# A new order for the first 12 blocks of an attention kernel: K is turned ahead of x, and q products stand between scores

## The chip, the cores and the metric

The kernel runs on one core of one Trainium2 chip. The metric is the device time of one execution in microseconds. "PE" is TensorE, "PEld" its weight loads, "DVE" VectorE, "ACT" ScalarE, "POOL" GpSimd, and "SP" SyncE, which here only issues DMAs.

## The reference

Everything is bf16 at the border, with 2048 tokens of width 640 and 32 heads of size 192. Only the last 512 keys and values of each head are used.

```python
xn = _layernorm(x)                                    # (1, 2048, 640)
q = (xn @ wq).reshape(1, 2048, 32, 192).transpose(0, 2, 1, 3)
k, v = k_cache[:, :, -512:, :], v_cache[:, :, -512:, :]
p = softmax(einsum("bhqd,bhkd->bhqk", q, k) * 192 ** -0.5)
o = einsum("bhqk,bhkd->bhqd", p, v)
s = o.transpose(0, 2, 1, 3).reshape(1, 2048, 6144) @ wo
g = silu(B(xn, w_r, w_gate, w_up, w_down))            # adds a gated FFN to the 2 tokens with the largest xn @ w_r
return x + s * g
```

## The kernel before

The 32 heads are processed in 8 groups of 4 (`GROUP`), and a group in two pairs of heads. The tokens come in four quads of 512, which are four tiles of 128 tokens each. A step is (group, quad, pair), and a step has two blocks of 256 tokens, so there are 128 blocks. One block needs:

- **q** (`q_whole`, line 302, or `q_phase`, line 323): the q of a step, transposed, in three parts (c = 0, 1, 2) of five products each, since 640 = 5 x 128. An eviction to `qT` on DVE (line 313) or ACT (lines 315, 350, 352) scales each part. `q_whole` uses all 128 rows of PE at once. `q_phase` and all the products below use 64-row halves, two at a time.
- **Scores** (`scores`, line 358): six products for one 128-token tile (a = 0 or 1) and both heads, `S` for short. The tile takes one of two PSUM buffers (`ps_s`).
- **Row maxima** (`row_max`, line 370, DVE) and **exponentials** (`exps`, line 375, ACT, one per head), `M` and `E`. A DMA on SP then transposes the exponentials into `pT`. A block whose number is in `SPLIT` (line 290) transposes each half by itself (line 381), another one both halves together after the second (line 383).
- **V products** (`o_item`, line 425): 32 products with `pT`, two evictions that divide by the row sums (lines 413 to 420, on the engines named, "v" for DVE and "a" for ACT), and a DMA transpose into `oT` (line 423). `P` for short.
- **Output products** (`w_item`, line 455): 24 products with `wo`, accumulated in `s_acc` (in the first group a copy, line 466 on ACT or 468 on DVE). `W` for short.

Before all of this, x is normalised. The first quad has tiles 0 to 3: statistics per half tile (`first_bn`, line 252), a square root on ACT (`first_dev`, 259), a reciprocal and the application on DVE (`first_apply`, 262). The later quads have `ln_parts` (line 486): statistics on DVE (`st`, line 496) or sums on ACT (`sa`, lines 507 and 511), then an inverse square root in steps (`nw`, lines 225 to 248: a logarithm and an exponential on ACT, one addition on POOL, three small steps on DVE, and the negated mean, line 197), and the application on ACT, DVE or POOL (`ap`, lines 189 to 194). Each tile is then turned by five PE products against an identity and evicted into `xnT` (`turn_tile`, line 279). The K of the first pair is turned on PE, too, in two parts of six products (`k_turn`, line 267). Later pairs have K reordered by a copy on POOL (`k_order`, line 118) and turned by a DMA (`k_transpose`, line 123). `wo` is loaded into one half of the partitions and doubled by a copy on POOL (`wo_double`, `wd`, line 148).

The order of all this is written out by hand: under `manual_schedule` (line 47) each engine executes its instructions in the order in which the program names them, and each DMA queue its DMAs. The kernel has 13 warming products on zeros (line 163). The first 12 blocks (`HEAD`, line 289) then follow the list of tokens `FIRST` (line 602), which `first` (line 528) carries out: `S.3.1` are the scores of block 3, tile 1, `q.2.1.a` is part 1 of step 2's q evicted on ACT, `P.1.va` the V products of block 1 with evictions on DVE and ACT, and so on. Blocks 12 and later follow one fixed pattern (`BLOCK`, line 946). The list ends with lines 999 to 1002.

The first loads stand ahead of the list: the first x tile and both heads' K on SP (lines 99 and 111), then x tiles 2 and 3 (line 157), and on ACT's queue x tile 1 and the first wq (lines 100 and 133).

## Time and profile before

| | us |
|---|---|
| median of 3 runs (lowest, highest) | 792.52 (791.92, 792.92) |
| the profiled execution | 793.03 |
| its span, first to last instruction | 791.3 |
| PE busy | 777.6 |
| DVE busy | 579.0 |
| ACT busy | 527.9 |
| POOL busy | 338.8 |

The profiled execution is one single execution, so its times belong together; it is 1.73 us longer than its span. Times in views of the trace count from the start of the span. In a timeline row the columns are start, duration, engine, line, operation, output<-inputs, number of instructions, and in brackets how long the engine was idle before it and what ended that. SPq and ACTq are issues of DMAs. A row of DMA issues has the queue, the number, the size of each, and the median time from issue to landing. A row of windows has the stretch and its length, the busy time of PE, PEld, DVE, ACT and POOL with the number of instructions, the granted clock of PE, the busy share of the DMA engines and GB/s.

### The profile page before, as it was taken

How to read it: one execution, taken by the hardware profiler on the slowest of the kernel's cores; microseconds unless marked ns; L12 is line 12 of the kernel's file. 1: busy time of each engine (PE TensorE's matmuls, PEld its weight loads, DVE VectorE, ACT ScalarE, POOL GpSimd, SP SyncE). 2: the span in 40 equal slices, each digit the busy share in tenths (PEclk: the TensorE clock that was granted, in tenths of full speed). 3: DMA queues.
4: the chain of work that ended last, by engine and by line, in shares of the span. 5: the costliest groups of instructions: out<-in, count | busy, mean ns of one | idle time of the engine just before them, and what ended most of it. 6: DMA issues, size and time to landing. Idle time of an engine off the chain costs nothing.

```text
span 791.3 us, 26980 instructions
## 1 busy us (share of the span) xinstructions
PE 777.6 (98%) x11356; PEld 571.5 (72%) x11356; DVE 579.0 (73%) x1069; ACT 527.9 (67%) x954; POOL 338.8 (43%) x280
## 2 busy tenths in 40 slices
PE   8899999999999999999999999999999999999997
PEld 4457677777777777777777777777777777777775
DVE  7898788877777776767776766766766766776775
ACT  5676666667666677767666666766666666666662
POOL 1334110023110226626120101569977795256895
PEclk9999999999999999999999999999999999999999
DMA  9989999899999999999999999999999999999992
GB/s 231 199 175 170 175 190 167 141 189 164 174 193 186 179 200 199 184 174 195 179 195 198 190 206 191 159 190 188 159 171 185 148 180 183 185 171 167 187 186 84
DMA packets 447130, 142.18 MB, mean 180 GB/s; under 512 B 414180, under 2 KB 446438, under 8 KB 447008
## 3 DMA queue, kind: packets, MB, share of 16 engines
q1 hardware_dynamic: 437312, 130.88, 99.7%
q10 hardware_dynamic: 8672, 6.72, 3.3%
q0 software_dynamic: 1024, 2.85, 1.3%
q8 instruction: 89, 1.46, 0.8%
q14 instruction: 33, 0.27, 0.1%
HBM read 40.31 MB, written 2.63 MB: 54 GB/s over the span
## 4 chain that ended last, share of the span: by engine, by line
PE 89%; DMA 4%; DVE 3%; ACT 2%; issue 1%; SPq 0%; DVEq 0%; ACTq 0%
PE w L447 24%; PE q_ps L340 23%; PE o_ps L406 20%; PE s L367 19%; DMA oT<-o_sb 2%; DVE nm L372 2%; ACT pexp L377 1%; PE q_ps L309 1%; DMA x_in<-in_A_x_dram 1%; DMA pT<-pexp 1%; DMA v_sb<-in_A_v_cache_dram 1%; DMA xsT<-xsel 0%; DVE fin_o L475 0%; PE tp L282 0%; PE gu_ps L787 0%
## 5 line engine op out<-in xcount | busy, mean ns | idle before, releaser
L372 DVE TENSOR_REDUCE nm<-s 128x2 f32<-128x1024 f32 x256 | 312.9, 1223 | 137.8 <-PE s L367 136.1
L377 ACT ACTIVATE pexp<-s,nm 128x512 bf16<-128x512 f32 x512 | 324.1, 688 | 95.3 <-DVE nm L372 91.0
L340 PE MATMUL q_ps<-xnT,wq_g 64*128 64x512 bf16 (+1 forms) x2340 | 232.4, 323 | 0.0
L447 PE MATMUL w<-wo_g,oT 64*128 64x320 bf16 x3072 | 231.5, 296 | 0.2
L367 PE MATMUL s<-kT,qT 64*128 64x512 bf16 x1536 | 211.4, 376 | 2.5 <-ACT pexp L377 1.7
L447 PEld LDWEIGHTS <-oT 64*128 64x128 bf16 x3072 | 169.1, 94 | 59.7 <-DMA oT<-o_sb 1.4
L406 PEld LDWEIGHTS <-pT 64*128 64x128 bf16 x4096 | 177.3, 94 | 31.4 <-issue 2.8
L406 PE MATMUL o_ps<-v_sb,pT 64*128 64x193 bf16 x4096 | 195.3, 243 | 2.9 <-DMA pT<-pexp 1.8
L420 ACT ACTIVATE o_sb<-o_ps,rl 128x192 bf16<-128x192 f32 x250 | 91.6, 418 | 133.6 <-DVE rl L413 128.3
L340 PEld LDWEIGHTS <-wq_g 64*128 64x128 bf16 x2340 | 125.5, 99 | 46.1 <-DVE qT L313 0.5
L151 POOL COPY wo_g<-wo_g 64x1920 bf16<-64x1920 bf16 x32 | 57.4, 1797 | 189.4 <-DMA wo_g<-in_A_wo_dram 188.5
L367 PEld LDWEIGHTS <-qT 64*128 64x128 bf16 x1536 | 84.5, 94 | 57.6 <-DVE qT L313 3.0
L470 DVE TENSOR_TENSOR s_acc<-s_acc,w 128x320 f32<-128x320 f32 x192 | 84.9, 484 | 31.8 <-PE w L447 31.7
L352 ACT ACTIVATE qT<-q_ps 128x1024 bf16<-128x1024 f32 x114 | 92.4, 811 | 7.4 <-PE q_ps L340 1.4
L417 DVE TENSOR_TENSOR o_sb<-o_ps,rl 128x384 bf16<-128x384 f32 x131 | 73.0, 557 | 4.5
L121 POOL COPY k_perm<-k_raw 128x768 bf16<-128x768 bf16 x30 | 24.2, 827 | 95.4 <-DMA k_raw<-in_A_k_cache_dram 68.7
L877 POOL TENSOR_SCALAR yh<-y_bc,oh 128x640 f32<-128x640 f32 x32 | 60.3, 1886 | 5.4 <-DMA y_bc<-y_d 2.6
L878 POOL TENSOR_TENSOR xn<-xn,yh 128x640 bf16<-128x640 bf16 x32 | 45.0, 1406 | 2.7
L864 POOL TENSOR_TENSOR tz<-tz,xn 128x640 f32<-128x640 f32 x16 | 22.4, 1400 | 54.2 <-ACT tz L863 54.2
L413 DVE RECIPROCAL rl<-o_ps 128x2 f32<-128x2 f32 x256 | 30.5, 160 | 12.2 <-PE o_ps L406 7.6
L937 POOL TENSOR_TENSOR s_acc<-s_acc,x_fin 128x640 f32<-128x640 f32 x16 | 22.4, 1400 | 11.0 <-DMA x_fin<-in_A_x_dram 10.1
L865 POOL TENSOR_TENSOR xn<-tz,xn 128x640 bf16<-128x640 f32 x16 | 22.4, 1398 | 1.3
(138 smaller groups left out, 275.9 us busy)
## 6 DMA issues: line engine op xcount, KB each, us to landing
wo_g<-in_A_wo_dram SPq DMA_DIRECT2D x32, 240.0 KB, 4.2
k_raw<-in_A_k_cache_dram SPq DMA_DIRECT2D x32, 192.0 KB, 3.3
v_sb<-in_A_v_cache_dram SPq DMA_DIRECT2D x32, 192.0 KB, 4.1
wq_g<-in_A_wq_dram SPq DMA_DIRECT2D x14, 288.0 KB, 3.7
pT<-pexp SPq DMA_TRANSPOSE x246, 4.2
wq_g<-in_A_wq_dram SPq DMA_DIRECT2D x14, 192.0 KB, 3.1
x_fin<-in_A_x_dram SPq DMA_DIRECT2D x16, 160.0 KB, 3.8
oT<-o_sb SPq DMA_TRANSPOSE x126, 3.6
```

What stands on the lines that cost most here:

```text
L151: nc.gpsimd.tensor_copy(out=grp[g][("wo", pr)][half(1), cs, :], in_=grp[g][("wo", pr)][half(0), cs, :])
L340: mm = nc.tensor.matmul(q_ps[k][:, 0:n] if type(q_ps) is list else q_ps[:, k, 0:n], lhsT=wq[half(r), dc, c:2 * Dh:3], rhs=xnT[half(r), tok ...
L352: nc.scalar.activation(out=out, in_=q_ps[:, :, 0:n], func=ACT.Copy, scale=scale)
L367: nc.tensor.matmul(s_of[b, a][:, r, :], lhsT=qT_of[i][half(r), c, u * P:(u + 1) * P], rhs=grp[g][("kT", pr)][half(r), :, c, :], start=(c = ...
L372: rm = nc.vector.tensor_reduce(out=nm_of[b, a], in_=s_of[b, a], axis=AX.X, op=ALU.max, negate=True)
L377: nc.scalar.activation(out=p_ring[:, b % 2, a, :, hh, :].rearrange("p (x j) e -> p x j e", x=2), in_=s_of[b, a][:, hh, :].rearrange("p (j ...
L406: nc.tensor.matmul(o_of[b][r][:, a, 0:Dh + 1], lhsT=pT_ring[half(r), b % RP, a, k, :], rhs=v_ring[half(r), (g * PAIRS + pr) % RV, k, 0:Dh ...
L417: nc.vector.tensor_tensor(out=o_sb, in0=src, in1=rl[:, r].unsqueeze(2).unsqueeze(3).to_broadcast([P, 2, 3, HK]), op=ALU.mult)
L420: nc.scalar.activation(out=o_sb[:, a], in_=src[:, a], func=ACT.Copy, scale=rl[:, r, a:a + 1])
L447: nc.tensor.matmul(w_ps[r][:, 0:HD], lhsT=oT_ring[half(r), bs[pr] % RT, c, :], rhs=grp[g][("wo", pr)][half(r), c, cs], start=(pr == 0 and ...
L470: nc.vector.tensor_tensor(out=acc, in0=acc, in1=src, op=ALU.add)
L877: nc.gpsimd.tensor_scalar(out=yh, in0=M["y_bc"][:, j, :], scalar1=M["oh"][:, n, j:j + 1], scalar2=None, op0=ALU.mult)
```

## The change

Only the first 12 blocks are touched. The first loads become tokens of the list (`lx`, `lk`, `lq`): SP issues x tiles 0, 2, 3 and wq, and ACT's queue x tile 1 and the two halves of K. In the list, K's turns (`kturn`) come ahead of the first two x tiles' turns. The statistics of tiles 2 and 3 come earlier. Many q products of steps 0 to 3, in parts of five, stand between two scores, where they stood in runs of 10 or 15 products. Evictions change engines: 4 of q, 2 of turned x tiles, 6 of the output products and one of two of a V product go from DVE to ACT; one application of the normalisation leaves ACT and one leaves DVE, and POOL takes both. Loads, copies and statistics stand at other places in the list, `wd.0` (the first doubling of `wo`) ahead of the last steps of the second quad's inverse square root among them. Whether a block's transposes are split is said by its token (`E.4.0.s`) and remembered in `split_of`: blocks 0 to 4 and 8 among the first 12, where it was 0 to 3; blocks 12 to 126 stay split. The number of products on each shape is the same.

```diff
@@ -96,8 +96,6 @@
         nc.sync.dma_start(out=x_in[t5][:, ts, :], in_=x_v[:, t5 * 4 + ts.start:t5 * 4 + ts.stop, :])
 
     x_in[0] = xin_pool.tile([P, 4, D], BF16, name="x_in")
-    nc.sync.dma_start(out=x_in[0][:, 0, :], in_=x_v[:, 0, :])
-    nc.scalar.dma_start(out=x_in[0][:, 1, :], in_=x_v[:, 1, :])
 
     grp = defaultdict(dict)
 
@@ -149,12 +147,6 @@
         pr, part = divmod(c, 2)
         cs = slice(part * 3, part * 3 + 3)
         nc.gpsimd.tensor_copy(out=grp[g][("wo", pr)][half(1), cs, :], in_=grp[g][("wo", pr)][half(0), cs, :])
-
-    for hh in range(2):
-        k_piece(0, 0, hh, nc.sync)
-    wq_piece(0, 0, 0, nc.scalar)
-    for n in (2, 3):
-        nc.sync.dma_start(out=x_in[0][:, n, :], in_=x_v[:, n, :])
 
     idle = late.enter_context(tc.tile_pool(name="idle", bufs=1)).tile([P, W], BF16, name="idle")
     nc.vector.memset(idle, 0.0)
@@ -287,7 +279,6 @@
     NS = len(steps)
     NB = 2 * NS
     HEAD = 12
-    SPLIT = (0, 1, 2, 3, *range(HEAD, NB - 1))
     qT_of = {}
     fin_x = {}
     fin_pool = {}
@@ -372,12 +363,16 @@
         rm = nc.vector.tensor_reduce(out=nm_of[b, a], in_=s_of[b, a], axis=AX.X, op=ALU.max, negate=True)
         last_max["ins"], last_max["S"] = rm.ins, s_no[b, a]
 
-    def exps(b, a):
+    split_of = set()
+
+    def exps(b, a, split=False):
         for hh in range(2):
             nc.scalar.activation(out=p_ring[:, b % 2, a, :, hh, :].rearrange("p (x j) e -> p x j e", x=2),
                                  in_=s_of[b, a][:, hh, :].rearrange("p (j e x) -> p x j e", j=NJ, x=2),
                                  func=ACT.Exp, bias=nm_of[b, a][:, hh:hh + 1], scale=1.0)
-        if b in SPLIT:
+        if a == 0 and split:
+            split_of.add(b)
+        if b in split_of:
             nc.sync.dma_start_transpose(out=pT_ring[:, b % RP, a], in_=p_ring[:, b % 2, a].rearrange("p k h e -> p (k h e)"))
         elif a == 1 and b < NB - 1:
             nc.sync.dma_start_transpose(out=pT_ring[:, b % RP].rearrange("p a k t -> p (a k) t"),
@@ -520,6 +515,7 @@
 
     ln = {t5: ln_parts(t5) for t5 in range(1, NT5)}
     copies = {"a": nc.scalar.copy, "v": nc.vector.tensor_copy}
+    queues = {"s": nc.sync, "a": nc.scalar}
 
     def flush(k):
         for f in mid.pop(k, []) + loads.pop(k, []) + bg.pop(k, []) + end.pop(k, []):
@@ -530,7 +526,13 @@
         op, *n = token.split(".")
         e = n[-1] if n and n[-1].isalpha() else None
         n = [int(c) for c in n if not c.isalpha()]
-        if op == "bn":
+        if op == "lx":
+            queues[e].dma_start(out=x_in[0][:, n[0], :], in_=x_v[:, n[0], :])
+        elif op == "lk":
+            k_piece(0, 0, n[0], queues[e])
+        elif op == "lq":
+            wq_piece(0, 0, n[0], queues[e])
+        elif op == "bn":
             first_bn(*n)
         elif op == "dev":
             first_dev(*n)
@@ -587,7 +589,7 @@
         elif op == "M":
             row_max(*n)
         elif op == "E":
-            exps(*n)
+            exps(*n, split=e == "s")
         elif op == "q":
             q_whole(n[0], n[1], n[2] if len(n) > 2 else None, e)
         elif op in ("qa", "qb"):
@@ -600,23 +602,19 @@
             flush(n[0])
 
     FIRST = """
-    v.0 x.1.0 bn.0.0 bn.1.0 x.1.1 bn.1.1 dev.1 bn.0.1 app.1 dev.0 k.1.0 app.0 bn.2.0 turn.0.a bn.3.0 bn.3.1 turn.1.a v.1 kturn.av bn.2.1 wq.1 dev.3 q.0.2.0.a k.1.1 q.0.0.0.v dev.2 v.2 q.0.1.0.a
-    ko.1 app.2 app.3 st.1.0
-    S.0.0 M.0.0 exp x.2 turn.2.a turn.3.a S.0.1 kT.1 M.0.1 st.1.1 E.0.0 st.1.2 wo.0 q.0.1.1.a q.0.0.1.a q.0.2.1.v E.0.1
-    S.1.0 wo.1 st.1.3 st.1.4 S.1.1 M.1.0 st.1.5 E.1.0 q.1.1.a M.1.1 q.1.2.a E.1.1 st.1.6 q.1.0.v st.1.7 nw.1.0
-    S.2.0 nw.1.1 nw.1.2 M.2.0 wo.2 S.2.1 nw.1.3 nw.1.4 nw.1.5 M.2.1 nw.1.6 st.2.0 E.2.0 ap.7.g ap.6.v P.0.vv E.2.1
-    S.3.0 M.3.0 ap.4.a v.3 S.3.1 turn.6.a ap.5.g wd.0 turn.5.a turn.4.v turn.7.v E.3.0 st.2.1 st.2.2 P.1.va M.3.1 wo.3 st.2.3 E.3.1 q.2.1.a q.2.2.v st.2.4 wd.1 q.2.0.v P.2.va
-    S.4.0 M.4.0 S.4.1 E.4.0 x.3 M.4.1 st.2.5 q.3.1.a E.4.1 wd.2 st.2.6 st.2.7 nw.2.0 q.3.2.a nw.2.1 nw.2.2
-    S.5.0 M.5.0 nw.2.3 E.5.0 nw.2.4 q.3.0.v S.5.1 wd.3 nw.2.5 sa.3.0.0 nw.2.6 M.5.1 E.5.1 sa.3.2.0 W.0.v ap.10.g
-    S.6.0 ap.11.g M.6.0 gk.0 E.6.0 ap.9.g ap.8.v W.1.v P.3.av S.6.1 M.6.1 P.4.va
-    S.7.0 st.3.6 E.6.1 turn.10.v turn.11.v turn.9.a turn.8.v sa.3.0.1 M.7.0 S.7.1 E.7.0 gk.1 q.4.2.v gq.0 q.4.1.v q.4.0.a
-    qa.5.0.1 sa.3.1.0
-    S.8.0 M.7.1 go.0 E.7.1 st.3.7 gw.0 sa.3.2.1 sa.3.1.1 nw.3.0 nw.3.1 M.8.0 W.2.v qb.5.0.1 nw.3.2 nw.3.3 nw.3.4 nw.3.5 P.5.av S.8.1 M.8.1 gq.1 nw.3.6 E.8.0 E.8.1 P.6.va ap.15.v
-    qa.5.2 ap.12.v
-    S.9.0 S.9.1 M.9.0 ap.14.g turn.12.v turn.14.v E.9.0 ap.13.g qb.5.2 turn.13.v M.9.1 turn.15.v
-    S.10.0 gT.0 E.9.1 gk.2 gk.3 P.7.vv W.3.v M.10.0 E.10.0 S.10.1 gv.0 P.8.vv W.4.a
-    qa.6.0.1 M.10.1 gd.0
-    S.11.0 E.10.1 M.11.0 B.11 go.1 E.11.0 W.5.v qb.6.0.1 P.9.av q.6.2.v S.11.1 M.11.1 E.11.1 gw.1 gv.1
+    lx.1.a lx.0.s lx.2.s bn.1.0 lx.3.s bn.1.1 lq.0.s lk.0.a lk.1.a bn.0.0 dev.1 v.0 bn.0.1 x.1.0 bn.2.0 dev.0 app.0 app.1 bn.3.0 bn.2.1 kturn.av turn.0.a k.1.0 turn.1.a v.1 k.1.1 q.0.0.0.a dev.2 wq.1 bn.3.1 q.0.1.0.v x.1.1 app.2 v.2 st.1.0 q.0.2.0.a ko.1
+    S.0.0 dev.3 exp turn.2.a app.3 kT.1 turn.3.v M.0.0 x.2 E.0.0.s S.0.1 q.0.2.1.a q.0.0.1.a st.1.1 M.0.1 st.1.2 q.0.1.1.a q.1.0.a E.0.1 st.1.3
+    S.1.0 q.1.2.a S.1.1 wo.0 st.1.4 M.1.0 st.1.5 E.1.0.s q.1.1.a M.1.1 st.1.6 wo.1 E.1.1
+    S.2.0 wo.2 st.1.7 nw.1.0 nw.1.1 nw.1.2 M.2.0 nw.1.3 nw.1.4 S.2.1 M.2.1 v.3 wd.0 nw.1.5 nw.1.6 st.2.0 ap.5.g ap.7.v E.2.0.s E.2.1 ap.6.v P.0.va
+    S.3.0 st.2.1 ap.4.g wo.3 turn.7.a turn.6.a st.2.2 S.3.1 M.3.0 turn.5.a turn.4.a M.3.1 P.1.va q.2.0.a E.3.0.s q.2.2.v st.2.3 st.2.4 q.2.1.v E.3.1 wd.1 P.2.va
+    S.4.0 S.4.1 x.3 M.4.0 E.4.0.s M.4.1 st.2.5 st.2.6 st.2.7 E.4.1 wd.2 q.3.1.a nw.2.0 q.3.2.a nw.2.1
+    S.5.0 M.5.0 E.5.0 nw.2.2 q.3.0.v S.5.1 wd.3 M.5.1 sa.3.0.0 nw.2.3 E.5.1 nw.2.4 nw.2.5 sa.3.0.1 W.0.v nw.2.6 ap.8.g
+    S.6.0 ap.11.g sa.3.2.0 ap.9.g gk.0 W.1.a M.6.0 S.6.1 M.6.1 E.6.0 P.3.vv E.6.1 P.4.va st.3.6 turn.11.v ap.10.g gk.1
+    S.7.0 turn.8.v turn.9.a turn.10.v S.7.1 sa.3.2.1 M.7.0 q.4.0.a E.7.0 q.4.2.a M.7.1 q.4.1.v st.3.7 qa.5.0.1 sa.3.1.0 E.7.1
+    S.8.0 sa.3.1.1 nw.3.0 W.2.a go.0 nw.3.1 nw.3.2 M.8.0 qb.5.0.1 nw.3.3 gq.0 nw.3.4 nw.3.5 nw.3.6 P.5.av
+    S.8.1 gw.0 E.8.0.s ap.14.g M.8.1 E.8.1 ap.15.v P.6.va ap.12.g qa.5.2 S.9.0 M.9.0 S.9.1 turn.12.v E.9.0 ap.13.g gk.2 turn.14.v qb.5.2 M.9.1 turn.15.a turn.13.v E.9.1 gT.0
+    S.10.0 M.10.0 E.10.0 gq.1 P.7.vv S.10.1 W.3.a P.8.av gk.3 M.10.1 W.4.v qa.6.0.1 S.11.0 E.10.1 M.11.0 W.5.a qb.6.0.1
+    B.11 E.11.0 gw.1 P.9.va gv.0 q.6.2.a gv.1 gd.0 S.11.1 M.11.1 E.11.1 go.1
     """.split()
 
 
@@ -959,7 +957,7 @@
             elif token[0] == "M":
                 row_max(b, int(token[1]))
             elif token[0] == "E":
-                exps(b, int(token[1]))
+                exps(b, int(token[1]), split=True)
             elif token == "W":
                 w_item(b - LAG)
             elif token == "P":
@@ -980,7 +978,7 @@
         elif op == "M":
             row_max(*n)
         elif op == "E":
-            exps(*n)
+            exps(*n, split=n[0] < NB - 1)
         elif op == "P":
             o_item(n[0], e)
         elif op == "O":
```

## The prediction

> **What bounds the kernel now.** First the page: how full each engine is, and the time of the execution.
>
> ```profile
> span 791.3 us, 26980 instructions
> PE 777.6 (98%) x11356; PEld 571.5 (72%) x11356; DVE 579.0 (73%) x1069; ACT 527.9 (67%) x954; POOL 338.8 (43%) x280
> ```
>
> TensorE (PE) is busy 98% of the span, and the change adds and removes no product. It can only gain or lose time in which PE waits. So the second view is PE's waits, here for the first 100 us, which hold the first 12 blocks.
>
> ```profile
> PE s L367 <- ACT pexp L377: 1.7, 4, 0.8
> PE o_ps L406 <- DMA pT<-pexp: 1.2, 1, 1.2
> PE q_ps L309 <- ACT xnT L283: 0.8, 2, 0.4
> PE s L367 <- ACT rstd L260: 0.6, 1, 0.6
> PE o_ps L406 <- DVE xnT L283: 0.6, 1, 0.6
> PE o_ps L406 <- DMA v_sb<-in_A_v_cache_dram: 0.5, 1, 0.5
> ```
>
> The columns are total, times, longest. Together 5.4 us (left out: the first 1.2, before any instruction had data). That is the idle time after a product has ended; the third view, PE's timeline, gives what a wait costs in starts.
>
> ```profile
> 1.19 5.73 PE L163 MATMUL warm_ps<-idle 128*128 128x512 bf16 x13 [1.19 <-DVE idle L160]
> 6.98 0.73 PE L282 MATMUL tp<-ident,xn 128*128 128x128 bf16 x10
> 7.58 0.83 PE L276 MATMUL tp_k<-ident,k_raw 128*128 128x128 bf16 x12
> 8.81 1.80 PE L309 MATMUL q_ps<-xnT,wq_g 128*128 128x256 bf16 x15 [0.41 <-ACT xnT L283]
> 11.21 0.92 PE L367 MATMUL s<-kT,qT 64*128 64x512 bf16 x6 [0.60 <-ACT rstd L260]
> ...
> 36.71 1.53 PE L367 MATMUL s<-kT,qT 64*128 64x512 bf16 x12
> ...
> 40.45 0.82 PE L367 MATMUL s<-kT,qT 64*128 64x512 bf16 x6
> 41.20 1.26 PE L309 MATMUL q_ps<-xnT,wq_g 128*128 128x512 bf16 x5
> 42.40 0.82 PE L367 MATMUL s<-kT,qT 64*128 64x512 bf16 x6
> 43.05 1.79 PE L447 MATMUL w<-wo_g,oT 64*128 64x320 bf16 x24
> ...
> 53.22 0.82 PE L367 MATMUL s<-kT,qT 64*128 64x512 bf16 x6 [0.44 <-ACT pexp L377]
> ...
> 84.61 1.26 PE L340 MATMUL q_ps<-xnT,wq_g 64*128 64x512 bf16 x10
> ```
>
> Between 8.81 and the next start, 15 products of 256 columns take 0.109 each though one lasts 0.27; the tail of about 0.16 overlaps, so a wait costs about 0.16 more than its idle figure. Block 12's products begin at 84.61, and from there both kernels have the same list. Three stages serve for the sum: up to the first score (11.21), on to block 4's (36.71), on to block 12 (84.61).
>
> What makes PE wait in the second stage is VectorE (DVE) and ScalarE (ACT): the windows give PE 3.98 of 5 us busy beside DVE 4.82.
>
> ```profile
> 10.00:15.00 5.00, 3.98 (x37) 2.24 (x36) 4.82 (x12) 4.47 (x9) 0.82 (x1) 1.00 1.13 265
> ```
>
> **The change, part by part. First loads.** Seven loads stand before the first q product. Their order, and microseconds from issue to landing (last column):
>
> ```profile
> 1.19 1.35 SPq L111 DMA_DIRECT2D k_raw<-in_A_k_cache_dram  x2
> 2.58 1.09 SPq L157 DMA_DIRECT2D x_in<-in_A_x_dram  x2
> 1.18 0.47 ACTq L133 DMA_DIRECT2D wq_g<-in_A_wq_dram  x1
> x_in<-in_A_x_dram ACTq DMA_DIRECT2D x1, 160.0 KB, 3.2
> wq_g<-in_A_wq_dram ACTq DMA_DIRECT2D x1, 480.0 KB, 5.4
> k_raw<-in_A_k_cache_dram SPq DMA_DIRECT2D x1, 192.0 KB, 5.5
> x_in<-in_A_x_dram SPq DMA_DIRECT2D x1, 160.0 KB, 5.4
> ```
>
> K's second half, issued near 1.9, lands at 7.4; the third x tile (2.58) at 8.0, the fourth (near 3.2) at 8.6, and then all 1504 KB are in. Afterwards SP issues x0, x2, x3, wq and ACT x1, K, K. K's second half is again issued near 1.85: 1.85 + 5.5 gives 7.4, I take **7.5**. Early bound: it has 160 KB less ahead of or beside it than now (1024 against 1184), and 160 KB are the 0.6 between the last two landings: 6.9. Late bound: last of the seven, 8.6 to 8.8. wq, issued near 2.2, plus 5.4 is 7.6; x2 and x3, issued near 1.2 and 1.7 ahead of everything large, come by the 3.2 of the first tile or a little more, at 4.8 and 5.4, some 3 us earlier than now.
>
> **K turned ahead of x.** Now the x tiles are turned at 6.98, while K lands, and K at 7.58. Afterwards PE has nothing between the end of the warming products (6.93) and K (7.5). Then 12 K products and 10 x products at 0.056 end at 8.8. ACT evicts half of K and both x tiles in a row.
>
> ```profile
> 7.47 1.29 ACT L283 COPY xnT<-tp 128x640 bf16<-128x640 bf16 x2 [1.28 <-PE tp L282]
> 8.65 0.82 ACT L277 COPY kT<-tp_k 128x768 bf16<-128x768 bf16 x1
> ```
>
> SP's next K load waits for the K turns to free their one buffer, with V, wq and x queued behind it on SP; the turns end within 0.2 us of now, so nothing moves there. The first six K turns are through at 8.05 (6 x 0.056 and a tail of 0.2); 0.7 for K, 0.6 and 0.7 for the tiles gives 10.05. The first q starts at 10.1 (now 8.81), 15 x 0.109 end at 11.75, the first score starts at 11.8. **Stage one: +0.6.**
>
> **Stage two.** The statistics of x2 and x3 come with their earlier data ahead of the scores, into time in which DVE waits for loads. 13 evictions and one normalisation leave DVE (4 of q, 1 of o, 2 of x, 6 of the output sum); the evictions go to ACT, which gives up one normalisation too, and POOL takes two. Hand-followed along the new lists with the durations of the rows, PE's waits are: q's third part at the first score 0.1, tile 2's normalisation 0.6, scores 0.1 + 0.6 + 0.7 + 0.1 (on q's eviction and the row maximum before), tile 7 1.4 to 2.0, first V products after it 0.2: 4.2. Now the view of waits has 4.0 here in seven waits (1.3 on the exps, 1.2, 0.4, 0.6, 0.5), 1.1 more for seven tails, and some 0.4 in waits too short for it: 5.5. So -1.3. Cutting the q products into fives between scores costs: the score at 40.45 and the q five after it take 0.75 and 1.20, where the score before w takes 0.65 and five at 0.216 1.08; every change between 128-row and 64-row products costs 0.1. The first 12 blocks have 23 such changes, the new list 29, four of the six here: +0.4. **Stage two: -0.9.**
>
> The 1.4 to 2.0 at tile 7 is the one new wait. The copy of wo on POOL is moved ahead of the last statistic steps. In the trace such a step beside such a copy was held:
>
> ```profile
> 42.16 1.78 POOL L151 COPY wo_g<-wo_g 64x1920 bf16<-64x1920 bf16 x1
> 42.72 1.23 DVE L241 SCALAR_TENSOR_TENSOR nw_a<-rstd 128x4 f32<-128x4 f32 x1
> 62.40 0.16 DVE L241 SCALAR_TENSOR_TENSOR nw_a<-rstd 128x4 f32<-128x4 f32 x1 [0.62 <-ACT rstd L235]
> ```
>
> 1.23 against 0.16, and it ends with the copy. I count one such hold of 1.1; bounds 0 and 1.8 (a whole copy). Behind the held step stand tiles 6 and 7's normalisations, their turns on PE, and the scores of block 3. [...]
>
> **Stage three.** The x turns of tiles 8 to 11, 20 in one run ahead of the score at 53.22, are parted by a score, so its wait goes (0.44 and a tail: 0.6); the held step of 42.72 stands elsewhere, which takes 0.4 of short waits along. Removed 1.0, left 0.2, two changes of shape 0.2. **Stage three: -0.6.** Moved at no cost: SP's pT transposes of blocks 4 and 8 in halves (two are issued in 2.64, a whole one in 2.77); the loads of group 1 a block earlier or later, under products; evictions to ACT, 67% busy on the page. If such a cover is gone, a PE wait of the kind in the view comes back, 0.4 to 0.8 once.
>
> ```profile
> 41.91 2.77 SPq L383 DMA_TRANSPOSE pT<-pexp  x1
> 23.40 2.64 SPq L381 DMA_TRANSPOSE pT<-pexp  x2
> pT<-pexp SPq DMA_TRANSPOSE x1, 4.7
> pT<-pexp SPq DMA_TRANSPOSE x1, 3.2
> ```
>
> **Sum:** 0.6 - 0.9 - 0.6 = **-0.9 us**. The profiled execution took 793.03, 1.73 more than its span, and lies 0.5 over the median 792.52; the sum is set on the median: **791.7**. Unknown: K's landing, 8.8 instead of 7.5 turns -0.9 into +0.4, earlier than 7.5 gives nothing (q then waits for wq and the evictions); the hold, none gives -1.2; the landing of pT, 3.2 to 4.7 by the last two rows, -1.1 to +0.1. Together -2.0 to +1.4.
>
> **Rivals.** (1) *The change doesn't do what it says:* K is turned first in PE's list, but not earlier, because its 192 KB yield to x and wq. For it: wq and K's first half were issued within 0.01 us of each other, and K, with 40% of the bytes, did not land before it (5.6 against 5.4). Against: by 7.4 K was in with 1184 KB. Time +0.4: **793.0**.
>
> (2) *Faster:* the hold does not fall on the statistics and the transposes land in 3.2, so tile 7 costs nothing: 1.4 more off, about -2.0: **790.6**. For it: the step at 62.40, with no copy beside it, took 0.16. Against: in the new lists step and copy stand side by side.
>
> (3) *Slower:* PE's clock falls back at the start. Early products ran at half speed: 13 of 512 columns in 5.73 us are 0.43 each, against 0.216 for the q five. At the end of the trace the clock fell again:
>
> ```profile
> 780.42 5.06 PE L447 MATMUL w<-wo_g,oT 64*128 64x320 bf16 x72
> 788.00:789.00 1.00, 0.00 (x0) 0.00 (x0) 0.45 (x1) 0.00 (x0) 0.00 (x0) 0.79 0.27 82
> 789.00:791.30 2.30, 0.00 (x0) 0.00 (x0) 0.00 (x0) 0.00 (x0) 0.00 (x0) 0.50 0.13 39
> ```
>
> The last product ended at 785.5, and the granted clock went to 0.5 some 3.1 us later. In the new list PE has only 22 short turns between 6.93 and 10.1. If these do not keep the clock, it decides at a gap of about 3.1 us, which K at 7.5 just reaches and K at 8.8 exceeds. Price: 15 q products +1.6, score and turns +0.8, the next q run in part: 2 to 4 on top of +0.4: **795.5**. Against: in the trace PE also has only turns from 6.98 to 8.81 and runs on at full speed. [...]
>
> **How the numbers follow.** Forecast 0.47 (own range 791.0 to 792.6), rival 1 0.18, rival 2 0.20, rival 3 0.15. A measurement here tells about 0.2% (1.6 us) from no change: faster is below 790.9, slower above 794.1. Faster: rival 2 but for its weak end, 0.18, and the forecast's early tail, 0.03: **0.21**. Slower: rival 3 and a little of 1: **0.18**. Same: **0.61**. The range takes in rivals 1 and 2 and leaves out most of 3: **790.3 to 794.2**.
>
> **What would show it.** Right: K's turns near 7.5, first q near 10.1, first score near 11.8, block 4 near 36.4, block 12 near 83.7, no 1.2 us wait on pT; a DVE step of about 1 us beside a POOL copy near 27, and PE waiting for tile 7's turn. Wrong: K after 8.5; q products of 256 columns above 0.109 (the clock); a wait on pT or V that stays; block 4 early but block 12 late, which would put the error into stage three.

## The result, and the profile after

The changed kernel takes **797.13 us** (median of 6 runs, 795.00 to 798.29) against 792.07 (6 runs, 791.66 to 792.92): a ratio of 1.0053, with a 95% interval of 1.0039 to 1.0067. It is 5 us slower, where -0.9 was forecast, and lies above the range of 790.3 to 794.2.

The page of the changed kernel: PE is busy 98%, as before, but for 1.8 us more, with the same number of products.

```profile
span 795.1 us, 26988 instructions
PE 779.4 (98%) x11356; PEld 573.9 (72%) x11356; DVE 575.1 (72%) x1055; ACT 531.6 (67%) x967; POOL 340.0 (43%) x282
```

PE's waits in the first 100 us of the changed kernel (total, times, longest):

```profile
PE tp_k L268 <- DMA k_raw<-in_A_k_cache_dram: 2.2, 1, 2.2
PE tp L274 <- DVE xn L185: 1.9, 2, 1.4
...
PE q_ps L300 <- ACT xnT L275: 0.8, 1, 0.8
PE w L442 <- ACT o_sb L415: 0.8, 1, 0.8
```

The waits that the change was to remove (on `pT`, on V, on the tile evictions ahead of V products) are gone. In their place stand a wait for K, one for the normalised tiles 7 and 6, and one that the kernel before does not have at all, for a V product's eviction. PE's timeline of the changed kernel shows where they lie:

```profile
1.19 5.39 PE L155 MATMUL warm_ps<-idle 128*128 128x512 bf16 x13 [1.19 <-DVE idle L152]
8.82 0.83 PE L268 MATMUL tp_k<-ident,k_raw 128*128 128x128 bf16 x12 [2.24 <-DMA k_raw<-in_A_k_cache_dram]
9.48 1.23 PE L274 MATMUL tp<-ident,xn 128*128 128x128 bf16 x10
11.55 3.36 PE L300 MATMUL q_ps<-xnT,wq_g 128*128 128x256 bf16 x15 [0.84 <-ACT xnT L275]
14.84 1.46 PE L358 MATMUL s<-kT,qT 64*128 64x512 bf16 x6
...
30.84 0.45 PE L274 MATMUL tp<-ident,xn 128*128 128x128 bf16 x5 [1.44 <-DVE xn L185]
...
39.88 1.46 PE L358 MATMUL s<-kT,qT 64*128 64x512 bf16 x12
...
86.98 1.26 PE L331 MATMUL q_ps<-xnT,wq_g 64*128 64x512 bf16 x10 [0.15 <-ACT qT L306]
...
95.53 1.81 PE L442 MATMUL w<-wo_g,oT 64*128 64x320 bf16 x24 [0.76 <-ACT o_sb L415]
```

K is turned at 8.82 (forecast 7.5). The 15 q products take 3.36 where the same products took 1.80 before: PE's clock is at half. Windows of the changed kernel, cut where the clock changed, show it in the granted clock (third column from the right):

```profile
6.11:9.53 3.42, 1.18 (x15) 0.74 (x14) 2.28 (x8) 0.30 (x2) 0.00 (x0) 1.00 1.15 232
9.53:12.94 3.41, 2.57 (x20) 2.04 (x17) 1.17 (x3) 2.03 (x4) 0.00 (x0) 0.50 0.88 186
12.94:16.35 3.41, 3.41 (x18) 1.42 (x16) 1.95 (x6) 1.82 (x5) 1.68 (x2) 0.50 1.06 297
16.35:19.77 3.42, 3.42 (x33) 2.47 (x33) 2.69 (x5) 2.22 (x4) 0.00 (x0) 1.00 1.17 173
```

Full, half for two windows of 3.41 us, full again. In the first of them PE was busy 1.18 of 3.42 us, 35%. The same stretch of the kernel before:

```profile
6.93:10.35 3.42, 2.96 (x37) 2.75 (x37) 2.14 (x6) 2.50 (x5) 0.00 (x0) 1.00 1.12 288
```

By stages, with the starts of the first score, of block 4's, of block 12's products and the span:

| | before | forecast | after | after - before |
|---|---|---|---|---|
| stage one, ends at | 11.21 | 11.8 | 14.84 | +3.6 |
| stage two takes | 25.50 | -0.9 | 25.04 | -0.5 |
| stage three takes | 47.90 | -0.6 | 47.10 | -0.8 |
| the rest takes | 706.7 | 0 | 708.1 | +1.4 |

Of the last 1.4, 0.9 lies between the first scores of blocks 13 and 14 (6.82 instead of 5.88), and 0.5 behind them. So the loss seems to sit in the first 15 us, and a little behind block 12. The experiments show that this reading is only half right.

### The profile page after: what moved, and what is told of

Read it like the earlier page. It is cut to its first block, busy times and chain, and to the rows that moved or that the text cites. A ratio compares the mean times of both kernels' runs of the same rounds, so it can differ in the third digit from the quotient of the medians.

```text
span 795.1 us, 26988 instructions
## 1 busy us (share of the span) xinstructions
PE 779.4 (98%) x11356; PEld 573.9 (72%) x11356; DVE 575.1 (72%) x1055; ACT 531.6 (67%) x967; POOL 340.0 (43%) x282
## 3 DMA queue, kind: packets, MB, share of 16 engines
q0 software_dynamic: 1024, 2.85, 1.2%
## 4 chain that ended last, share of the span: by engine, by line
PE 93%; DMA 3%; DVE 2%; ACT 2%; issue 1%; ACTq 0%; DVEq 0%
PE w L442 25%; PE q_ps L331 23%; PE o_ps L401 20%; PE s L358 20%; PE q_ps L300 2%; DMA k_raw<-in_A_k_cache_dram 1%; DMA oT<-o_sb 1%; DMA pT<-pexp 1%; ACT pexp L370 1%; PE tp L274 1%; DVE nm L363 1%; DMA xsT<-xsel 0%; ACT o_sb L415 0%; DVE fin_o L470 0%; PE gu_ps L785 0%
```

## The experiments

All 18 are variants of the two lists. "The old order from X" means: the tokens of the changed list up to X, then what is left in the order of the kernel before. Starts are from one profiled execution each: of the first score, of block 4's, and the time from block 13's first score to block 14's. From there to the end all profiles have the same instructions and still take 692.3 to 694.7 us, a spread that no run explains, so the text goes by starts, and by times only where the ratios differ clearly. Each ratio is against the kernel before on the same chip (its median is 791.9 to 793.5 there); several chips were used, so medians of two variants are compared with care. "Half" counts executions with a mean granted clock of 0.997 or less: one half-clock window takes 3.41 x 0.5 / 791 = 0.0022 off the mean. It can miss a window: e8's profiled execution had one and a mean of 0.998. The kernel before had 3 such executions of 162, the changed one 6 of 6.

| run | median | ratio [95%] | first score | block 4 | block 13 to 14 | half |
|---|---|---|---|---|---|---|
| before | | | 11.21 | 36.71 | 5.88 | |
| after | 797.13 | 1.0053 [1.0039, 1.0067] | 14.84 | 39.88 | 6.82 | 6 of 6 |
| e1_warm21 | 795.91 | 1.0041 [1.0026, 1.0056] | 12.47 | 39.16 | 6.85 | 5 of 6 |
| e2_old_loads | 795.31 | 1.0030 [1.0020, 1.0041] | 12.19 | 39.26 | 7.00 | 9 of 12 |
| e3_before_new_loads | 794.46 | 1.0024 [1.0013, 1.0035] | 11.09 | 37.82 | 5.89 | 7 of 12 |
| e4_old_head | 795.15 | 1.0024 [1.0012, 1.0037] | 10.57 | 38.67 | 5.90 | 7 of 11 |
| e5_wd_late | 793.57 | 1.0015 [1.0003, 1.0026] | 15.59 | 39.83 | 5.90 | 6 of 12 |
| e6_old_head_wd_late | 794.12 | 1.0025 [1.0014, 1.0036] | 10.86 | 36.73 | 5.90 | 4 of 12 |
| e7_wd_late_old_tail | 793.51 | 1.0010 [0.9995, 1.0025] | 11.86 | 36.06 | 5.88 | 9 of 12 |
| e8_before_wd_early | 792.78 | 1.0002 [0.9991, 1.0013] | 10.79 | 38.81 | 5.88 | 1 of 12 |
| e9_wd_tail_warm21 | 793.05 | 1.0013 [1.0000, 1.0026] | 13.54 | 37.76 | 5.88 | 2 of 12 |
| e10_wd_tail_old_loads | 791.62 | 0.9997 [0.9987, 1.0008] | 11.98 | 36.75 | 5.88 | 3 of 11 |
| e11_wd_tail_old_loads_warm17 | 791.64 | 0.9997 [0.9988, 1.0006] | 12.11 | 36.48 | 5.88 | 1 of 11 |
| e12_wd_warm21 | 794.31 | 1.0028 [1.0016, 1.0039] | 14.13 | 38.58 | 7.16 | 0 of 6 |
| e13_before_warm5 | 794.97 | 1.0026 [1.0016, 1.0036] | 12.18 | 39.24 | 5.89 | 2 of 11 |
| e14_early_copy_back | 793.70 | 1.0004 [0.9993, 1.0015] | 12.01 | 38.28 | 5.88 | 8 of 11 |
| e15_new_tail_back | 793.33 | 1.0007 [0.9993, 1.0020] | 12.03 | 36.80 | 7.15 | 1 of 12 |
| e16_best | 791.80 | 0.9978 [0.9964, 0.9992] | 11.21 | 35.99 | 5.88 | 0 of 12 |
| e17_x_ahead_of_k | 791.86 | 0.9973 [0.9958, 0.9987] | 10.26 | 36.77 | 5.89 | 0 of 12 |
| e18_gw_late | 792.20 | 1.0006 [0.9994, 1.0019] | 12.11 | 36.31 | 5.90 | 2 of 12 |

### The start: e1 to e4

The first theory was the prediction's third rival, the clock at the start; its own rival was that K and wq are only late.

**e1**: more warming products.

```diff
-    for _ in range(13):
+    for _ in range(21):
```

> The changed kernel with 21 warming products in place of 13, so that PE multiplies until about 8.4 us, when K's second half lands. Clock theory (the granted clock halves because PE has only turns, no other products, for one whole window of 3.4 us): the clock stays at 1.00 past 9.5, the 15 q products take 1.8 instead of 3.4, the first score starts at 13.3 instead of 14.84, block 4's at 37.6 instead of 39.88, and the time falls by 2.0 to 2.6 us, to about 794.8. Lateness theory (only the late K and wq cost, the clock is a by-product): q still takes over 3 us, the first score at 14.8, time 797.1.

**e2**: the first loads as before.

```diff
-    lx.1.a lx.0.s lx.2.s ... lx.3.s ... lq.0.s lk.0.a lk.1.a
+    lx.0.s lx.1.a lk.0.s lk.1.s lq.0.a lx.2.s lx.3.s
```

> The changed kernel with the first loads as before (x0, both K halves, x2, x3 on SP; x1 and wq on ACT's queue), K still turned ahead of x. All theories: K's second half at 7.4, wq at 7.6. If turns do not hold the clock up: PE has no other product from 6.6 to 10.1, so the clock still halves between 9.5 and 10.4, q takes 3 us or more, the first score starts near 13, time about 795.5. If turns count as work, or only lateness matters: the clock stays at 1.00, q from 10.1 at 0.109 each, the first score at 11.8, time about 793.7, and the landing of K was the whole failure of the prediction.

**e3**: the kernel before with its first loads as in the first of these two lines.

> The kernel before with only the new order and queues of the first loads (x still turned ahead of K). K's second half lands at 8.7, wq at 10.1, as in the changed kernel. Clock theory: x turns at 7.0, K turns at 8.8, no other product from 6.6 to 10.2, so the clock halves, q takes 3 us or more, first score at 13.5, about 2.5 slower than the kernel before, 794.6. Lateness theory: q starts at 10.2 at full speed, first score at 12.3, about 1.1 slower, 793.2.

**e4**: the old list up to `S.0.0`, then what is left in the new order.

> The kernel before up to its first score (its loads, its turns, its first q), and from there the changed order. Theory one (all of the loss is the first stage; the rest of the new order gains): first score at 11.2, block 4's at 36.3, block 12's products at 83.4, time 1.3 below the kernel before, 790.8. Theory two (the new order of blocks 9 to 11 hands block 12 a wait on an eviction of a V product, 0.8 to 1.4 us, that takes the gain back): the same milestones up to block 12, then PE waits for an o eviction 8 to 11 us after it, time 792.1, no difference.

In e1 and e2 the clock held at the start, and the first score came 2.4 and 2.7 us earlier than in the changed kernel. But block 4's score came only 0.7 and 0.6 earlier, and e4, with a start that is better than that of the kernel before, is 2 us late at block 4. No theory expected that: most of what is gained at the start is lost ahead of block 4. The timeline of e4 shows it:

```profile
27.20 1.78 POOL L149 COPY wo_g<-wo_g 64x1920 bf16<-64x1920 bf16 x1 [5.82 <-DMA wo_g<-in_A_wo_dram]
29.09 1.72 POOL L185 TENSOR_SCALAR xn<-x_in,rstd,nmr 128x640 bf16<-128x640 bf16 x2
30.01 0.54 PE L274 MATMUL tp<-ident,xn 128*128 128x128 bf16 x5 [2.46 <-POOL xn L185]
```

And the windows of e4, laid on its clock's changes:

```profile
26.82:30.24 3.42, 0.96 (x10) 0.35 (x10) 2.79 (x4) 1.18 (x3) 2.93 (x3) 1.00 1.18 255
30.24:33.65 3.41, 3.09 (x37) 2.48 (x36) 0.00 (x0) 1.39 (x2) 3.35 (x3) 0.50 1.30 232
```

POOL's copy of `wo` (`wd.0`) stands ahead of POOL's two normalisations. It waits 5.82 for its load, they wait behind it, and PE waits 2.46 for them. PE is then busy only 0.96 of 3.42 us, and in the next window its clock is at half. In the changed kernel the copy holds a step of DVE instead, as the prediction had it (timeline of the changed kernel):

```profile
27.57 1.78 POOL L149 COPY wo_g<-wo_g 64x1920 bf16<-64x1920 bf16 x1 [1.53 <-DMA wo_g<-in_A_wo_dram]
28.61 0.76 DVE L239 SCALAR_TENSOR_TENSOR rstd<-nw_a,rstd 128x4 f32<-128x4 f32 x1
```

In e1 the copy came earlier and held it for longer (timeline of e1):

```profile
25.50 1.78 POOL L149 COPY wo_g<-wo_g 64x1920 bf16<-64x1920 bf16 x1 [2.00 <-DMA wo_g<-in_A_wo_dram]
26.07 1.23 DVE L239 SCALAR_TENSOR_TENSOR rstd<-nw_a,rstd 128x4 f32<-128x4 f32 x1
27.82 1.81 DVE L185 TENSOR_SCALAR xn<-x_in,rstd,nmr 128x640 bf16<-128x640 bf16 x2
28.77 0.45 PE L274 MATMUL tp<-ident,xn 128*128 128x128 bf16 x5 [1.92 <-DVE xn L185]
```

PE's two waits for tiles 7 and 6 are 2.4 together in e1, 1.9 in the changed kernel: 0.5 more. Behind them e1's clock is at half from 30.04 to 33.45, where the changed kernel's stays full, and from the second of these turns to the next q products e1 takes 4.77 instead of 3.43. So in these two profiles the gain of 2.4 at the first score shrinks to 0.7 mostly by the clock.

e3 has the first score as early as the kernel before and loses 1.1 until block 4, by a wait of 2.1 on `pT` where that had 1.2, and a half-clock window behind it; neither theory named this. The new loads alone cost 0.24%.

### The copy of wo: e5, e6, e8, e14

**e5**: the changed kernel with one token moved.

```diff
-    ... S.2.1 M.2.1 v.3 wd.0 nw.1.5 nw.1.6 st.2.0 ap.5.g ... S.3.0 st.2.1 ap.4.g wo.3 ...
+    ... S.2.1 M.2.1 v.3 nw.1.5 nw.1.6 st.2.0 ap.5.g ... S.3.0 st.2.1 ap.4.g wd.0 wo.3 ...
```

> The changed kernel with one token moved: the first copy of wo on POOL stands behind POOL's normalisations of tiles 5 and 4, not ahead of the last Newton steps. Copy theory (this copy holds a DVE step and POOL's own normalisations, PE waits for tiles 7 and 6 with little but turns to do, and in some executions its clock then halves for a window): the DVE step near 26 to 28 takes 0.16 instead of 0.8 to 1.2, PE's waits on DVE's xn in stage two fall from 1.9 to 2.4 to below 0.5, from block 3's score to block 4's takes 10 or less instead of 11.3 to 13.1, no half-clock window between 26 and 36, time 2 to 3 us less than the changed kernel: 794.5. Start theory (the half clock and the late loads of the first 15 us are the loss): block 3 to block 4 gets shorter by 0.6 at most, time 796.5 or more.

**e6**: e4 with the same move.

> The kernel with the old start (up to the first score) and the changed order after it, with the same token moved. Copy theory: PE's wait of 2.8 for POOL's xn goes, the half-clock window at 30 with it, block 4's score at 36.3 instead of 38.67, time 792.5 (795.15 without the move). If the new order has another wait behind it (DVE's row maxima, the transposes of block 0 and 1): block 4's score at 37.5 or later, time 794 or more.

**e8**: the kernel before with `wo.0` behind `S.1.1` and `wd.0` behind `M.2.1`.

> The kernel before with the suspect alone: the first load of wo stands behind block 1's second score (two blocks later) and its copy on POOL behind block 2's second row maximum, ahead of the last Newton steps and of POOL's normalisations, as in the changed kernel. Copy theory: PE waits 2 to 3 us for POOL's or DVE's xn ahead of the turns of tiles 4 to 7, block 4's score at 38.5 instead of 36.71, a half-clock window behind it in some executions, time 794.3 to 795.5. Start theory: DVE and POOL have slack there, block 4 at 37 or earlier, time within 0.5 of the kernel before.

**e14**: e11 (below) with `wd.0` put back ahead of `nw.1.5`.

> The run with old loads, 17 warming products and the old order from block 10, with the copy of wo put back ahead of the last Newton steps. Copy theory: PE waits 1.9 to 2.8 for tiles 7 and 6 again, from block 3's score to block 4's 13.1 instead of 10.65, a half-clock window behind the wait (mean granted clock 0.997 or less) in more than half of the executions, time 794.0 (791.64 without). Rival (in this order the copy costs its wait alone, since the share before it stays above 0.4): 792.9 and clocks as without it.

e5: the step takes its normal time, and the copies follow the normalisations (timeline of e5).

```profile
29.22 0.15 DVE L239 SCALAR_TENSOR_TENSOR rstd<-nw_a,rstd 128x4 f32<-128x4 f32 x1
29.68 1.78 POOL L185 TENSOR_SCALAR xn<-x_in,rstd,nmr 128x640 bf16<-128x640 bf16 x2 [3.03 <-DVE nmr L189]
30.78 0.45 PE L274 MATMUL tp<-ident,xn 128*128 128x128 bf16 x5 [0.77 <-DVE xn L185]
31.53 5.23 POOL L149 COPY wo_g<-wo_g 64x1920 bf16<-64x1920 bf16 x3
```

From block 3's first score to block 4's it takes 10.65 instead of 11.31 (13.13 in e1), there is no half-clock window there, and the ratio falls from 1.0053 to 1.0015: about 3 us. The two profiled executions show 0.7 of it here and 0.9 between blocks 13 and 14 (see below); for the rest there is no trace. PE's wait is 1.2, not below 0.5 as expected, since DVE's two normalisations still take 0.9 each (1.75 for the two) beside POOL's (0.45 each in the first stage). In e14 the copy alone is put back into the best version: block 3 to 4 takes 12.64 instead of 10.64, 8 of 11 executions have a half-clock window instead of 1, and the median rises by 2.1 (the ratios differ by only 0.07%, inside their intervals). Its three executions at 0.999 took 790.67, 791.83 and 793.70, the eight others 792.88 to 794.23. The windows of e14:

```profile
24.90:28.31 3.41, 1.57 (x25) 0.81 (x20) 3.38 (x6) 1.96 (x4) 2.86 (x3) 1.00 1.21 255
28.31:31.72 3.41, 3.19 (x21) 1.62 (x22) 3.34 (x8) 1.91 (x4) 3.35 (x3) 0.50 1.31 208
```

e6 gained its wait back (block 4 at 36.73 instead of 38.67); it is no earlier than the kernel before, since PE waits 2.8 us on `pT` up to there. But the time did not follow: the ratios are 1.0025 and 1.0024, where 792.5 was expected. Why is open, since these waits lie ahead of block 4 and are in its 36.73. e8 was a **miss** in time: the suspect put into the kernel before cost nothing in the median. Its profiled execution has the wait and the half-clock window (block 4 at 38.81) and took 793.59, but only 1 of 12 executions was at 0.997 or less. So PE's wait behind the early copy is in every profile that has it (1.9 to 2.8, against 1.2 in e5), but its price in time is not one number: some 3 us from the changed kernel to e5, 0.6 by the ratios (2.1 by the medians) from e11 to e14, nothing from e4 to e6 and in e8. That it costs where it empties PE far enough for the clock to fall fits the profiles of e1, e2, e4 and e14; e6 and e8 keep it from being shown for the time.

### The last blocks: e7, e12, e15, e18

**e7**: e5 with the old order from `S.10.0`.

> As the run with the copy moved behind the normalisations, and from block 10 on the tokens in the order of the kernel before. Tail theory (the new order of blocks 10 and 11 hands block 13 a wait for an o eviction): from block 13's score to block 14's takes 5.9 instead of 6.8, time 0.9 below the run with the copy moved alone, 793.6. Rival (this wait comes from when the transposes happen to land, since the run with the old start had the new order of these blocks and took 5.9): no difference in the time beyond 0.3.

**e12**: e5 with 21 warming products; **e9**: e7 with 21.

> The copy late and 21 warming products, with the new order to the end of block 11. Against the run that has the old order from block 10 beside them: tail theory 1.0 slower (from block 13's score to block 14's 6.8 against 5.9, or the loss later), 792.2; rival (the order of blocks 10 and 11 is indifferent) equal within 0.4.

> The run with the copy late and the old order from block 10, with 21 warming products in place of 13. Share theory (the clock halves for a window of 3.41 us when PE was busy less than some 0.4 of the window before, turns included; with 13 products this happens at the start whenever K lands late, in 8 of 12 executions of the run without the extra products): no half-clock window before 17 us, mean granted clock 0.998 or more in nearly all executions, median 791.2 (the three executions at 0.998 or more of the run without them had 790.4 to 791.7), all within about 2 us. Lateness theory (K and wq land late, the clock adds nothing): median 793.5 as without them.

**e15**: e11 with the new order to the end.

> The run with old loads, 17 warming products and the copy late, with the new order to the end of block 11 again. Tail theory: a wait for an o eviction near block 13, 13's score to 14's 6.8 to 7.2 instead of 5.9, time 1.2 above 791.64. Rival (it depends on when the transposes land, since it was absent with the copy late and 13 warming products): 791.6 to 792.0.

e7 has the median of e5, as its rival said; the wait was absent from e5's profile already, and e7's executions spread over 6 us with the clock. e12 against e9, and e15 against e11, have the clock held in nearly all: the new order of blocks 10 and 11 costs 1.3 and 1.7 in the medians, 1.2 and 0.8 by the ratios, whose intervals overlap. From block 13's score to block 14's it takes 7.16 and 7.15 instead of 5.88. Going back to the old order also takes back engines of some evictions there. Yet e4, e5 and e6 have the new tokens, too, and take 5.90. The timelines tell why, first that of the changed kernel:

```profile
91.03 1.78 POOL L149 COPY wo_g<-wo_g 64x1920 bf16<-64x1920 bf16 x1 [2.86 <-DMA wo_g<-in_A_wo_dram]
91.39 2.10 DVE L672 SCALAR_TENSOR_TENSOR junk<-xn,wr_bc 128x640 bf16<-128x640 bf16 x1
94.56 0.22 DVE L408 RECIPROCAL rl<-o_ps 128x2 f32<-128x2 f32 x2
```

The same two instructions in e4:

```profile
90.19 0.81 DVE L672 SCALAR_TENSOR_TENSOR junk<-xn,wr_bc 128x640 bf16<-128x640 bf16 x1
90.21 2.44 POOL L149 COPY wo_g<-wo_g 64x1920 bf16<-64x1920 bf16 x1 [3.06 <-DMA wo_g<-in_A_wo_dram]
```

It is the same hold once more, between POOL's copy of group 1's `wo` (`gd.0`) and DVE's step for the router's score. Where the copy starts first, DVE's step takes 2.10 instead of 0.81, and the reciprocals of a V product, its eviction and PE's next output products are late. Where DVE starts first, by 0.02 us here, the copy is held (2.44 instead of 1.78), and PE does not wait. The order of these two starts goes with the wait in the changed kernel, e1, e12 and e15 (copy first) and in e4, e5 and e6 (DVE first). e2 has 7.00 although DVE started first: there the exponentials wait for a transpose, as the rival to the tail theory had it. From the timeline of e2:

```profile
97.45 1.27 ACT L370 ACTIVATE pexp<-s,nm 128x512 bf16<-128x512 f32 x2 [2.34 <-DMA pT<-pexp]
```

**e18**: e15 with the load that releases this copy at the end of the list.

```diff
-    B.11 E.11.0 gw.1 P.9.va gv.0 ... S.11.1 M.11.1 E.11.1 go.1
+    B.11 E.11.0 P.9.va gv.0 ... S.11.1 M.11.1 E.11.1 go.1 gw.1
```

> The run with the new order to the end of block 11 (old loads, 17 warming products, copy of the first wo late), with one load moved: the second part of group 1's wo, for which POOL's copy of that wo waits, is issued at the end of the list. Hold theory for the end of the list (this copy starts within 0.4 us ahead of DVE's step for the router score, which is held to the copy's end: 2.1 to 2.4 instead of 0.82, and the reciprocals of a V product behind it): the copy starts 4 us later, the step takes 0.82, from block 13's score to block 14's 5.9 instead of 7.15, time 791.9 (793.33 without the move, 791.64 with the old order from block 10). Order theory (the new places of the other tokens of blocks 10 and 11 make the wait): 6.8 or more, 793.3.

The copy now starts far behind the step (timeline of e18), and the wait is gone: 5.90. In time this is not shown: the median is 792.20 against e15's 793.33, but on another chip, and the ratios are 1.0006 and 1.0007.

```profile
87.82 0.81 DVE L672 SCALAR_TENSOR_TENSOR junk<-xn,wr_bc 128x640 bf16<-128x640 bf16 x1
...
93.75 1.78 POOL L149 COPY wo_g<-wo_g 64x1920 bf16<-64x1920 bf16 x1 [8.92 <-DMA wo_g<-in_A_wo_dram]
```

### Loads against clock: e9, e10, e11, e13

e9's expectation stands above: its first score comes at 13.54 with the clock at full throughout, 1.43 after that of e11. PE's timeline of e9:

```profile
9.24 0.83 PE L268 MATMUL tp_k<-ident,k_raw 128*128 128x128 bf16 x12 [0.60 <-DMA k_raw<-in_A_k_cache_dram]
...
11.81 1.80 PE L300 MATMUL q_ps<-xnT,wq_g 128*128 128x256 bf16 x15 [1.18 <-ACT xnT L275]
```

**e10**: e7 with the old loads; **e11**: e10 with 17 warming products.

> The run with the copy late and the old order from block 10, with the first loads on the queues and in the order of the kernel before, 13 warming products. If the late landing of K under the new queues is what lets the share fall: K's second half at 6.8 to 7.4, share of the first window after the warming products above 0.5, few executions below 0.997, median 792.0. If K ahead of x is enough by itself to empty PE: half-clock windows as often as with the new loads, median 793.5.

> The same with the old loads and 17 warming products, which end at 6.5 to 7.8. Share theory: no half-clock window at the start in any execution, first q near 10.3, median 791.2. Lateness theory: as with the old loads and 13 products.

**e13**: the kernel before with 5 warming products.

> The kernel before with 5 warming products in place of 13, nothing else: PE's clock should still be at half when the turns and the first q products come, with K and wq as early as before. It prices the half clock without late loads. Clock theory: the 15 q products take 3.4 instead of 1.8, the first score starts at 12.8 to 13.5 instead of 11.21, the clock is full by 17, time 2 to 2.5 above the kernel before. Rival (the later waits of the second stage, on row maxima and transposes, absorb a late start): first score just as late, block 4's score at 37.2 or earlier (36.71 before), time within 0.7 of it.

e9 had few half-clock windows (2 of 12 against 9 in e7), and its ratio was no better (1.0013 against 1.0010); its median of 793.05 is nearer the lateness theory's 793.5 than the share theory's 791.2. With the clock held K came no sooner (turns at 9.24 in e9, at 7.55 in e7), and what the half clock costs in the whole time these two runs don't show. At the first score the traces separate the two. From the start of K's turns to the first score it takes 4.30 in e9, 4.31 in e1 and e7, all with the clock full, and 6.02 in the changed kernel: 1.7 is the clock. Against the forecast of 11.8 the first score is 3.0 late, and the other 1.3 is K, whose turns begin at 8.82 instead of 7.5. The old loads cure both: K's second half lands at 6.86 (e10) and 6.97 (e11), and the ratio falls from 1.0010 to 0.9997, though the intervals overlap. With them, the extra warming products add nothing. e13 was to price the clock alone; with K and wq early, the 15 q products take 2.85 at partly half speed (PE's timeline of e13):

```profile
9.35 2.85 PE L309 MATMUL q_ps<-xnT,wq_g 128*128 128x256 bf16 x15
```

The first score is 1.0 late (the clock was full from 11.5, earlier than expected), and the kernel 0.26% slower, 2.1 us. Block 4's score is 2.5 late in the profile, 1.4 of it by a longer wait on `pT` (2.6 against 1.2) ahead of block 3; and a second half-clock window follows that wait (28.56 to 31.97). So the 2.1 us are not the price of the half clock at the start alone. Why the wait on `pT` grows with a late start stays open.

A late start was carried along in full where the copy is out of the way: e5 and e7 have the same tokens up to block 10, and in their profiled executions the first score differs by 3.73, block 4's by 3.77.

### What is left of the change: e16, e17

**e16**: e11 with 15 warming products, and the first statistic of tile 2 (which comes at 7.2 with the old loads) behind the normalisations of tiles 0 and 1.

```diff
-    ... x.1.0 bn.2.0 dev.0 app.0 app.1 bn.3.0 bn.2.1 kturn.av turn.0.a ...
+    ... x.1.0 dev.0 app.0 app.1 bn.2.0 bn.3.0 bn.2.1 kturn.av turn.0.a ...
```

> The run with old loads, the copy late and the old order from block 10, with 15 warming products (17 there) and one more token moved: the first statistic of x tile 2, for which DVE waits until 7.3, stands behind the normalisations of tiles 0 and 1. K is still turned ahead of x. If the x turns (8.8 to 9.4 there, the last to start q) are late because of this wait: first q at 9.5 instead of 10.3, block 4's score at 35.7 instead of 36.5, time 790.8 (791.64 there). If the tile normalisations of the second stage bind whatever comes before: block 4's score unchanged, 791.6.

**e17**: e16 with `turn.1.a turn.0.a` ahead of `kturn.av`, and with `app.1` ahead of `app.0`, so that tile 1 is normalised and turned first.

> As the run just described, but with both x tiles turned ahead of K, as in the kernel before: K's turn ahead of x is the only part of the title undone. If that part is worth something by itself: slower by 0.5 or more. If the two orders differ only in who waits (q for its x tile or the first score for K): first q at 8.9, first score 0.7 earlier, block 4's score within 0.2, time within 0.4.

PE's timeline of e16:

```profile
6.91 0.83 PE L268 MATMUL tp_k<-ident,k_raw 128*128 128x128 bf16 x12 [0.96 <-DMA k_raw<-in_A_k_cache_dram]
...
9.48 1.80 PE L300 MATMUL q_ps<-xnT,wq_g 128*128 128x256 bf16 x15 [1.18 <-ACT xnT L275]
...
35.99 1.46 PE L358 MATMUL s<-kT,qT 64*128 64x512 bf16 x12
```

First q at 9.48, as expected, block 4 at 35.99. The median of 791.80 is not the 790.8 that was expected, but the kernel before was slow on this chip, too (793.47, its highest median), so the ratio counts: 0.9978 [0.9964, 0.9992] of the time before, 1.7 us. e17 has 0.9973, and the intervals overlap almost wholly: **no gain or loss from turning K ahead of x is shown**, to within about 1 us. The profiles are less even. e17's first score comes 0.95 earlier than e16's and its block 4 0.78 later, since PE waits for the second piece of wq (timeline of e17), a wait that e16 does not have:

```profile
16.99 1.26 PE L300 MATMUL q_ps<-xnT,wq_g 128*128 128x512 bf16 x5 [1.87 <-DMA wq_g<-in_A_wq_dram]
```

## Why the prediction was wrong, step by step

In the two profiled executions the changed kernel is 3.8 us longer, 4.7 more than the forecast of -0.9. By stages: 3.0 up to the first score, 0.4 in the second stage, -0.2 in the third, 1.4 behind it.

- **First loads: failed, by size.** "I take 7.5" for K's second half: 8.68 in the profiled run, 7.07 to 9.69 in the seven profiles with the new loads. It stayed near its late bound of 8.8 in that run, but not in others (9.11, 9.25, 9.69). wq was taken at 7.6 without a bound and landed at 10.11, though in the changed kernel q then waited for ACT's evictions and not for wq. From the changed kernel's DMA issues, time to landing in the last column (before: 5.4 and 5.6; K's second half alone 6.8, before 5.5):

```profile
wq_g<-in_A_wq_dram SPq DMA_DIRECT2D x1, 480.0 KB, 8.0
k_raw<-in_A_k_cache_dram ACTq DMA_DIRECT2D x2, 192.0 KB, 5.8
```

  Adding the old latency to the new issue time assumed that the place in a queue does not matter. wq went from second on its queue to behind three tiles, and from 5.4 to 8.0.
- **K turned ahead of x: right in mechanism.** Where K landed about when it was assumed to (e7, turns at 7.55) the first q starts at 10.12 (forecast 10.1) and the first score at 11.86 (11.8). e10 and e11 come near these numbers by another way: K is earlier there, and PE waits for x instead.
- **The clock was put at nothing in the sum: the step that failed most.** Rival 3 happened, with rival 1's late K as its trigger, at 0.15 and 0.18 the two least likely cases (that K *yields* to x and wq is not shown). 1.7 of the 3.0 at the first score is the clock, 1.3 is K. The half clock reaches 1.5 us into the second stage, too, which can account for its 0.4. In e7, where both come and go together, three executions at 0.998 or more took 790.4 to 791.7, the other nine 792.4 to 796.2: the price of 2 to 4 was of the right size. Its condition, an estimate from the one gap of 3.1 us at the end of the trace, was wrong in form. In e2 PE had nothing but turns from 6.40 to 10.46, and the granted clock stayed at 1.00: the window from 5.73 to 9.15, with 17 turns and 0.66 us of warming products, had a share of 0.57.
- **The hold at tile 7: right wait, missing consequence.** The wait of 1.4 to 2.0 came (1.9 in two pieces), with a held step of 0.76 where 1.1 was counted. What was missing is that this wait, with little but turns behind it, took PE's share of a window to 0.30, 0.38, 0.28 and 0.46 in e1, e2, e4 and e14, and the granted clock to 0.50 in the next. The bound of 1.8 was for a held step; a copy that waits for its load ahead of POOL's normalisations (2.46 in e4) was not in the sum.
- **Stages two and three: about right.** The third gained 0.8 in the changed kernel itself (forecast 0.6), the second 0.5 (0.9). With the three faults out, e11 gains 1.13 in stage two (25.50 to 24.37) and 0.9 from there to block 12; but its copy is late, so its waits at tiles 7 and 6 are 1.2, not the 1.4 to 2.0 of the sum. The waits on `pT`, on V and at 53.22 did not come back.
- **"From there both kernels have the same list": failed.** The sum ended at block 12. POOL's copy of group 1's wo, released by a load that the change moved, reached into block 13: 0.9 to 1.3 in the profiles where it started ahead of DVE's step. The other 0.5 of the last 1.4 has no cause that a run shows.
- The three faults, undone one after the other, take the ratio from 1.0053 to 0.9997: the copy about 3 us (1.0053 to 1.0015), the last blocks 0.4 (e5 to e7), the loads 1.0 (e7 to e10). Only the first step is clear of the intervals, and in other orders the prices differ (1.2 for the last blocks from e12 to e9).
- Two slips in the working change nothing: 792.52 - 0.9 is 791.6, and rival 3's 2 to 4 on top of 793.0 has its middle at 796.

## What to carry to other kernels

Where an engine works in the order of the program, look not only at what an instruction costs where it is moved to, but at what it waits for. In e4 a copy that waited 5.82 for its load held up the two normalisations behind it, and PE by 2.46; in e1 one that ran beside a step of a neighbour engine went with 1.23 for that step, which took 0.15 in e5. Where PE was busy 0.46 of a window or less, the clock was at half in the next in nine of the ten cases below, so price the clock behind a wait, too, and follow a moved load to the end of the last instruction that it releases, not to the end of the edited list. Don't add an old latency to a new issue time when early loads change their places: the 480 KB of wq took 5.4 us (before) and 4.6 (e11) second on ACT's queue, and 8.0 (the changed kernel) and 7.1 (e5) behind three tiles on SP's.
